# Attention and low-rank mixer: the halves of an odd pair's product with values put closer together, both transposes of a couple asked for at once

## Chip, cores, metric

The kernel runs on one core of a Trainium2 chip. The metric is device time in microseconds (us), lower is better. All runs were of a granted TensorE clock (the share of full speed that the chip allowed) of 0.996 to 1.000 as the mean of a run.

## The reference, cut to what matters

```python
q_n = q / (norm(q) + 1e-06); k_n = k / (norm(k) + 1e-06)      # 8 batches, 12 heads, 448 rows, 64 wide
attn = softmax(q_n @ k_n.T / tau)
x = (attn @ v).transpose(0, 2, 1, 3).reshape(8, 448, 768)
u = x + (x.transpose(0, 2, 1) @ U @ V).transpose(0, 2, 1)       # rank 32
out = u + maximum(u @ w_ch1, 0) @ w_ch2                         # 768 -> 3072 -> 768
```

## The kernel before

TensorE works on pairs of heads, six to a batch: pair n is pair p = n mod 6 of batch b. From n = 14 on, two pairs (an even one and the odd one after it) make a couple. Between the steps of attention, the kernel puts pieces of the mixer of the batch before ("channel pieces", six matmuls each, taken from the list `fill`), so that TensorE never runs dry. `V(n, half)` is a half of the product with values and its division (the result is X), `A2` the product U^T X for a couple, `X2` the request for X's transpose, `T` the request for a transposed q and k, `S3` the last chunk of the scores.

```python
def spread(n, order, nf, first=0):
    weights = [w if fn is not False else 0 for w, fn in order]
    given = acc = 0
    for i, ((_, fn), w) in enumerate(zip(order, weights)):
        if fn:
            fn()
        for g in after.pop((n, i + first), []):
            g()
        acc += w
        want = nf * acc // sum(weights)          # whole pieces
        f(min(want - given, len(fill)))
        given = want
# ... (even pair of a couple)
order = [
    (3, lambda: (step_S3(*pairs[n]), Sc(n, 0, 1))),
    (2, lambda: V(n - 1, 0)),
    (3, lambda: (V(n - 1, 1), X2(n - 1))),
    (4, lambda: (A2(n - 2), Sc(n, 2), Sc(n + 1, 0), open_V(*pairs[n]))),
    (2, lambda: V(n, 0)),
    (3, lambda: (V(n, 1), X2(n))),
]
spread(n, order, int(round((len(fill) - KEEP) / (1 + (-p) % NP))))
# ... (where the norms of a later couple are made: reduce of q, reduce of k, root; then invert)
at = [(m - 3, 0), (m - 3, 0), (m - 3, 5)] + [(m - 2, i) for i in (0, 1, 2)]
when = (m - 2, 3)
# ... (accumulator banks of the channel pieces: two, in turn; U^T X takes the other one)
def own_bank():
    other = 1 - m_state["at"]
    if not m_state["open"]:
        m_state["at"] = other
    return bank_m(other)
# ...
def step_A2(b, p, apart):
    ap = own_bank()[:, 0:128] if apart else av_of[(b, p + 1, 1)][:, 384:512]
    # ... eight matmuls of U_sb and X, then
    nc.scalar.copy(out=A_of[(b, p)], in_=ap)
```

## Time and profile before

| | before |
|---|---|
| time, median of 4 runs | 579.82 us (579.45 to 580.06) |
| span of the profiled run | 578.5 us |
| TensorE busy | 567.5 us, 98% |
| VectorE, ScalarE busy | 212.9 us, 262.6 us |

The prediction below shows the lines that matter. In the wait lines, the columns are the engine and line that waited, what it waited for, then the sum, the number and the longest of such waits.

### The profile page before, as it was taken

To read this page: it belongs to the slowest core of one execution; us is meant where nothing else is said; L and a number is where in the kernel's file an instruction comes from. 1 tells how busy PE (TensorE), PEld (TensorE's weight loads), DVE (VectorE), ACT (ScalarE), POOL (GpSimd) and SP (SyncE) were. 2 spreads that over 40 slices of the span, in tenths; PEclk is the share of its full clock that TensorE was granted. 3 is DMA by queue.
4 is the path that set the end of the run, shared out by engine and by line. 5 is a ranking of instruction groups with operands and counts; after the bars stand their busy time and mean duration, and the time that the engine had idled before them with its cause. 6 is when DMAs were issued, how large, how long until landed. Compare 5 with 4: busy or idle time off the path is not lost.

```text
span 578.5 us, 12651 instructions
## 1 busy us (share of the span) xinstructions
PE 567.5 (98%) x5302; PEld 330.3 (57%) x5302; DVE 212.9 (37%) x460; ACT 262.6 (45%) x449; POOL 214.0 (37%) x202
## 2 busy tenths in 40 slices
PE   6999999999999999999999999999999999999997
PEld 6665566555655556555556555655565555655565
DVE  7874551433343324524234233333243331320011
ACT  5877544465333662445424555336433365214300
POOL 8756574724416236416145064244161420000000
PEclk9999999999999999999999999999999999999999
DMA  6899999686367565574465673674545612222022
GB/s 163 191 245 240 233 209 205 174 170 153 95 139 146 108 141 124 127 160 110 92 151 135 130 151 99 139 167 98 116 112 126 139 38 50 57 54 51 7 49 56
DMA packets 139882, 74.53 MB, mean 129 GB/s; under 512 B 86688, under 2 KB 139696, under 8 KB 139824
## 3 DMA queue, kind: packets, MB, share of 16 engines
q1 hardware_dynamic: 129568, 63.20, 48.9%
q0 software_dynamic: 9632, 10.01, 10.2%
q8 instruction: 41, 0.67, 0.5%
q10 hardware_dynamic: 624, 0.51, 0.3%
q14 instruction: 17, 0.14, 0.1%
HBM read 52.19 MB, written 11.01 MB: 109 GB/s over the span
## 4 chain that ended last, share of the span: by engine, by line
PE 83%; DMA 8%; DVE 3%; SPq 2%; POOL 1%; ACT 1%; issue 1%; POOLq 0%; DVEq 0%
PE mp L598 34%; PE mp L570 33%; PE sc L331 5%; DMA w_sb<-in_moe_w_ch_dram 5%; DMA kst<-in_k_dram 2%; PE av L419 2%; PE up L419 1%; PE av L393 1%; PE up L393 1%; PE av L343 1%; POOL sq L243 1%; SPq L315 1%; PE mp L508 1%; ACT E L356 1%; DVE ss L248 1%
## 5 line engine op out<-in xcount | busy, mean ns | idle before, releaser
L598 PE MATMUL mp<-w_sb,relu 128*128 128x384 bf16 (+2 forms) x1368 | 235.3, 323 | 0.3 <-DMA w_sb<-in_moe_w_ch_dram 0.3
L598 PEld LDWEIGHTS <-relu 128*128 128x128 bf16 x1368 | 126.1, 98 | 84.1 <-issue 9.6
L570 PEld LDWEIGHTS <-w_sb 128*128 128x128 bf16 x1128 | 105.8, 98 | 99.3 <-issue 7.2
L356 ACT ACTIVATE E<-sc 128x896 bf16<-128x896 f32 x144 | 125.1, 922 | 53.4 <-PE sc L331 52.4
L575 ACT ACTIVATE relu<-mp 128x448 bf16<-128x448 f32 x163 | 88.7, 544 | 122.1 <-PE mp L570 122.1
L268 POOL TENSOR_TENSOR qk<-kst,inv 128x512 bf16<-128x512 f32 x43 | 46.0, 1069 | 236.7 <-DVE inv L262 215.2
L570 PE MATMUL mp<-uO,w_sb 128*128 128x448 bf16 x576 | 113.6, 353 | 0.0
L570 PE MATMUL mp<-uE,w_sb 128*128 128x448 bf16 x552 | 111.9, 353 | 0.2 <-DMA w_sb<-in_moe_w_ch_dram 0.2
L617 DVE TENSOR_TENSOR o_sb<-mp,ut 128x384 f32<-128x384 f32 (+2 forms) x51 | 28.0, 550 | 140.1 <-PE mp L598 140.1
L248 DVE TENSOR_REDUCE ss<-sq 128x16 f32<-128x1024 f32 (+1 forms) x50 | 57.7, 1165 | 1.6 <-POOL sq L243 0.8
L577 DVE TENSOR_SCALAR relu<-mp 128x448 bf16<-128x448 f32 x25 | 15.6, 625 | 99.5 <-PE mp L570 99.0
L268 POOL TENSOR_TENSOR qk<-qst,inv 128x512 bf16<-128x512 f32 x44 | 47.4, 1079 | 1.7 <-PE up L480 1.7
L331 PE MATMUL sc<-qkT 64*64 64x448 bf16 x576 | 42.8, 360 | 0.6 <-ACT E L356 0.3
L243 POOL TENSOR_TENSOR sq<-kst 128x1024 f32<-128x1024 f32 (+1 forms) x23 | 42.7, 1857 | 1.6 <-DMA kst<-in_k_dram 1.4
L243 POOL TENSOR_TENSOR sq<-qst 128x1024 f32<-128x1024 f32 x21 | 39.8, 1893 | 7.3 <-DMA qst<-in_q_dram 6.3
L276 POOL CAST v<-vst 128x1024 bf16<-128x1024 f32 (+1 forms) x25 | 25.2, 1010 | 11.8 <-DMA vst<-in_v_dram 10.4
L419 PEld LDWEIGHTS <-E 128*128 128x128 bf16 x744 | 29.1, 97 | 0.0
L353 ACT ACTIVATE E<-av 128x448 bf16<-128x448 f32 x17 | 9.2, 541 | 42.4 <-PE up L343 21.8
L331 PEld LDWEIGHTS <-qkT 64*64 64x64 bf16 x576 | 12.8, 105 | 14.2 <-issue 8.6
L393 PEld LDWEIGHTS <-E 128*128 128x128 bf16 x408 | 17.3, 97 | 5.0
L419 PE MATMUL av<-v,E 128*128 128x65 bf16 x420 | 18.9, 193 | 0.0
L412 PEld LDWEIGHTS <-E 128*128 128x128 bf16 x124 | 11.4, 98 | 9.0 <-issue 0.8
(109 smaller groups left out, 364.9 us busy)
## 6 DMA issues: line engine op xcount, KB each, us to landing
out_dram<-o_sb SPq DMA_DIRECT2D x108, 96.0 KB, 2.2
w_sb<-in_moe_w_ch_dram POOLq DMA_DIRECT2D x8, 1152.0 KB, 18.4
qst<-in_q_dram SPq DMA_DIRECT2D x23, 256.0 KB, 3.9
vst<-in_v_dram SPq DMA_DIRECT2D x46, 128.0 KB, 2.8
kst<-in_k_dram SPq DMA_DIRECT2D x44, 128.0 KB, 2.9
qst<-in_q_dram SPq DMA_DIRECT2D x23, 192.0 KB, 4.0
vst<-in_v_dram SPq DMA_DIRECT2D x46, 96.0 KB, 2.7
kst<-in_k_dram SPq DMA_DIRECT2D x44, 96.0 KB, 2.8
```

The lines of the kernel that those rows point to most:

```text
L243: nc.gpsimd.tensor_mul(sq[:, 0:self.nh * 4, :], self.flat(t), self.flat(t))
L248: nc.vector.reduce_sum(self.ss[:, j, 0:self.nh * 4], self.sq[j][:, 0:self.nh * 4, :], axis=AX.X)
L268: eng.tensor_mul(qks[self.gi % 2][:, j, i, :, :, :], t[:, 2 * j:2 * j + 2, :, :].rearrange("p h c d -> p c h d"), iv.unsqueeze(3).to_broad ...
L276: nc.gpsimd.tensor_copy(out=self.flat(v65[self.s])[:, :, 0:D], in_=self.flat(vst[self.s]))
L331: nc.tensor.matmul(out=sc[o:o + 64, h, 0:S], lhsT=t[r, 1, c * 128 + o:c * 128 + o + 64], rhs=t[r, 0, 0:S], start=True, stop=True)
L356: nc.scalar.activation(out=e[:, 2 * c:2 * c + 2, 0:S], in_=sc[:, :, 0:S], func=AF.Exp)
L393: nc.tensor.matmul(out=av[:, ic, :], lhsT=e[:, 2 * c + h, ic * 128:(ic + 1) * 128], rhs=vv[:, 2 * j + h, c, :], start=False, stop=(ic == 3 ...
L419: nc.tensor.matmul(out=av[:, i, h, :], lhsT=e[:, 2 * c + h, ic * 128:(ic + 1) * 128], rhs=vv[:, 2 * j + h, c, :], start=False, stop=(i == ...
L570: nc.tensor.matmul(out=mp, lhsT=w1_sb[:, cc, f * 128:(f + 1) * 128], rhs=u[:, cc, 0:S], start=(cc == 0), stop=(cc == CC - 1))
L575: nc.scalar.activation(out=relu[:, f, o:o + S], in_=mp, func=AF.Relu)
L598: nc.tensor.matmul(out=mp, lhsT=relu[:, f, r0:r0 + 128], rhs=w2_sb[:, f, half * HC + c0:half * HC + c1], start=(f == 0), stop=(b > 0 and f ...
L617: nc.vector.tensor_add(o.rearrange("p (k d) -> p k d", d=128), mp.rearrange("p (k d) -> p k d", d=128), ut_of[(b, half)][:, c0 // 128:c1 / ...
```

## The change

The intent: a half of the odd pair's product with values should come sooner, so that its division on VectorE is done when U^T X needs X, with two channel pieces between them instead of one; and both transposes of a couple should be asked for together.

```diff
@@ requests for transposes
-            put(m - 1, -1 if first else 0, lambda m=m: T(m + 1))
+            put(m - 1, -1, lambda m=m: T(m + 1))
@@ order of an even pair
-                (2, lambda: V(n - 1, 0)),
-                (3, lambda: (V(n - 1, 1), X2(n - 1))),
+                (1, lambda: V(n - 1, 0)),
+                (4, lambda: (V(n - 1, 1), X2(n - 1))),
```

## The prediction

> **What bounds the kernel now.** I began with the page's busy table and its slices. They say that TensorE is never idle for long, at full granted clock, in all forty slices.
>
> ```profile
> PE 567.5 (98%) x5302; PEld 330.3 (57%) x5302; DVE 212.9 (37%) x460; ACT 262.6 (45%) x449; POOL 214.0 (37%) x202
> ...
> PEclk9999999999999999999999999999999999999999
> ```
>
> No other engine is above 45%, so only what stands in TensorE's own stream, or what its stream waits for, can move the end. Next I read the waits of TensorE. In the part that the change touches (from about 190 us on) there are only two kinds: two stalls of U^T X (L508) for X, and one of the scores for a transposed qkT.
>
> ```profile
> PE up L343 <- DMA qkT<-qk: 0.4, 1, 0.4
> PE mp L508 <- DVE X L431: 0.4, 2, 0.2
> ```
>
> These waits look like the aim of the change. Third, I opened the timeline around one of the two X stalls (columns: start, duration, engine, line, what, and in brackets the idle time before).
>
> ```profile
> 235.12 1.14 PE L598 MATMUL mp<-w_sb,relu 128*128 128x384 bf16 x6
> 235.88 1.21 DVE L248 TENSOR_REDUCE ss<-sq 128x16 f32<-128x1024 f32 x1
> 237.01 0.55 DVE L617 TENSOR_TENSOR o_sb<-mp,ut 128x384 f32<-128x384 f32 x1
> 237.47 0.17 DVE L430 RECIPROCAL rd<-up 128x4 f32<-128x4 f32 x1
> 237.66 0.29 PE L508 MATMUL mp<-X,U_sb 128*32 128x128 bf16 x6
> 237.68 0.42 DVE L431 TENSOR_TENSOR X<-up,rd 128x256 bf16<-128x256 f32 x1
> 238.16 0.23 PE L508 MATMUL mp<-X,U_sb 128*32 128x128 bf16 x2 [0.20 <-DVE X L431]
> 238.32 0.57 PE L331 MATMUL sc<-qkT 64*64 64x448 bf16 x8
> ```
>
> The last two of eight matmuls wait for the second half of X, which ends at 237.68 + 0.42 = 238.10; it was late because VectorE ran a reduce and the output addition (L617) first. From the first L508 to the scores it took 238.32 - 237.66 = 0.66 us. Where nothing waits (at 218.73) the same stretch takes 218.96 - 218.73 = 0.23. So one stall costs 0.43 us, not the 0.20 in the brackets, and the two together 0.86.
>
> **What the Trainium skill says.** "Perfetto Trace Analysis", Tensor Engine Instruction, says the recorded end of a matmul is a model, not a measurement; so I measure by starts alone. The trace agrees: six channel matmuls of 384 columns are recorded as 1.14 us, but start to start (235.12 to the next product's 236.10) they take 0.98. "PSUM — Partial Sum Buffer", Engine vs sequencer instructions, says that ScalarE's and VectorE's queues are strict FIFO and that matmuls start in program order. This trace agrees where L617 stands ahead of the division above. The same page, PSUM bank collisions raise a hardware error, advises guarding PSUM by bank: a product can't open a bank until the engine that empties it is done. That is the rule on which my prediction turns.
>
> **The change part by part.** I compared the two built programs, engine by engine, with their semaphores and wait values.
>
> *The transposes.* Asking for T(m+1) one place earlier gives no different program: with this line alone changed, every engine's instructions, semaphores and wait values are the same as before, because nothing else for the DMA queue stands between the two places. So it is worth 0, and the 0.4 us wait on qkT stays.
>
> *The halves.* The weights 2,3 become 1,4, but steps are whole numbers. With 9 steps to a pair (in even batches) the rounding gives the same order. With 7 steps (the mixer of the even batch before has 24 + 24 steps to spread over six pairs) it gives 0,2 channel pieces behind the halves in place of 1,1. The order of TensorE differs in eight places only, each moving one piece of six matmuls from between the halves to behind them. Call them by the pair p: p=2 in batches 3, 5, 7 (about 194, 330 and 466 us), p=4 in the same (216, 351, 488), p=0 in batches 4 and 6 (235, 370). No matmul is added or taken away, and the first quarter of the trace shows halves back to back without loss: their first matmuls at 22.70 and 23.20 are 0.50 apart, the same 0.50 that a half takes with a piece behind it (215.69 to 216.19). So without waits U^T X would start at the same time as before. What is left is what it waits for.
>
> It starts after two pieces, in the accumulator bank of the first of the two, so that piece must be emptied from the bank. Before, that first piece lay one half earlier. Now its emptying stands later in the queue of VectorE or ScalarE.
>
> (a) p=0, two places. VectorE now divides before L617. The division starts after the reduce, at 237.01, and its multiply 0.21 later at 237.22 (237.68 - 237.47); L617 follows 0.34 after that (238.02, the next instruction, less 237.68), at 237.56, and takes 0.56, to 238.12. The X stall is gone: X is whole by 237.64. But in the changed program the first L508 waits for L617. Instruction end to matmul start was 238.16 - 238.10 = 0.06, so it starts at 238.18, and the scores 0.23 later at 238.41, against 238.32 before. Loss 0.09; the other place (373.30) works out to 0.10. The wait for X has been swapped for one on the output addition; net **+0.2 us** for two, where 0.86 was to be saved.
>
> (b) p=2, three places. Here the pieces are of the first product and ScalarE empties the first with relu (L575). Before:
>
> ```profile
> 196.19 0.54 ACT L575 ACTIVATE relu<-mp 128x448 bf16<-128x448 f32 x1 [0.53 <-PE mp L570]
> ...
> 196.90 0.32 ACT L253 ACTIVATE ss<-ss,tiny 128x32 f32<-128x32 f32 x1 [0.16 <-DVE ss L248]
> ...
> 197.25 0.23 ACT L254 ACTIVATE ss<-ss 128x32 f32<-128x32 f32 x1
> ...
> 197.72 0.30 PE L508 MATMUL mp<-X,U_sb 128*32 128x128 bf16 x8
> ```
>
> In the changed program this relu stands behind L253 and L254, the square root of the norms, which waits for a VectorE reduce that does not move (ends 196.86). The piece itself would be done near 196.66, but relu has to stand in line: ScalarE's next instruction starts about 0.11 before the recorded end of the last (18.37 + 0.92 against 19.18), so relu runs from 197.37 to 197.91, and L508 starts 0.05 to 0.06 later at 197.96 instead of 197.72: loss 0.24. The places at 333.35 and 469.50 have the same distances. Three of them, **+0.7 us**.
>
> (c) p=4, three places. The pieces are quarters of one accumulation (L598) with nothing to empty between them; the reduce still holds the division, X still ends at 218.73 and the last two L508 still find it. **0**.
>
> All of it lies in TensorE's stream, which is full to the end, so it adds straight to the time: 0.2 + 0.7 = 0.9 us. 579.99 + 0.9 = **580.9 us**, 0.16% slower.
>
> **The rivals.** *The intended gain.* The two stalls for X go and nothing replaces them: 580.0 - 0.9 = 579.1. For it: the stalls are real, and VectorE does divide sooner. Against it: the wait values of the changed program put L617 before L508 and the root before relu. *Nothing at all*, 580.0: the eight shifts are absorbed. For it: each is a quarter of a microsecond and a run's spread was 0.6; against it: the only slack in the stream after these places is the one 0.4 us wait on qkT at 439. If a delayed TensorE gives that transfer time, up to 0.4 comes back, 580.5; but the transfer's queue follows TensorE's own output, so I expect both to shift together. *A cascade.* A_sb, the exponentials and the next half's inputs on ScalarE come 0.25 late, and the next products wait again, doubling (b): 581.7. Against it: these exponentials wait for the scores, which are late by the same amount, so distances are kept.
>
> **Range and chances.** The sizes are from one trace with an error of perhaps 0.1 us a place; a different chip or run moved the before kernel by 0.6. Low end just under half of the intended gain, high end the cascade: 579.5 to 581.7. A change of 2% would be 11.6 us, more than all of TensorE's idle time (578.5 - 567.5 = 11.0), so faster by 2% has practically no chance, and nothing adds so much either: 0.01, 0.98, 0.01.
>
> **What would show it.** Right: the wait of L508 for X is gone, with two of about 0.4 us for L617's o_sb and three of about 0.2 for relu L575 in its place; the wait of L343 for qkT still there; L508 to scores 0.23 in all eight places. Wrong, if no wait of L508 is listed and the span is shorter by most of 0.9; or if the p=4 places change; or if waits appear later, at L331, L393 or L419, which would be the cascade.

## The result

The changed kernel took 581.77 us, median of 4 runs (581.02 to 582.80), against 579.82 of before: 1.95 us more. The ratio was 1.0035, 95% interval 1.0015 to 1.0055. (A ratio is the mean time of one kernel's fast runs over that of the other's of the same rounds, so it is not quite the ratio of the medians.) The time is within 2% as forecast, but 581.77 lies above the range of 579.5 to 581.7, and the loss is about twice the 0.9 us predicted.

The busy time of TensorE did not move. First the page of the changed kernel, then TensorE's waits in it:

```profile
PE 567.5 (98%) x5302; PEld 330.7 (57%) x5302; DVE 213.0 (37%) x460; ACT 262.7 (45%) x449; POOL 214.1 (37%) x202
```

```profile
PE mp L570 <- DMA w_sb<-in_moe_w_ch_dram: 1.1, 1, 1.1
PE mp L598 <- DMA w_sb<-in_moe_w_ch_dram: 0.9, 1, 0.9
PE mp L508 <- DVE o_sb L617: 0.8, 2, 0.4
...
PE mp L508 <- ACT relu L575: 0.5, 3, 0.2
...
PE up L343 <- DMA qkT<-qk: 0.3, 1, 0.3
```

The third and fourth lines are the predicted ones: the two waits for X have gone, two for the output addition and three for relu have come. The first two were not in the prediction. In the kernel before the same two waits are short:

```profile
PE mp L598 <- DMA w_sb<-in_moe_w_ch_dram: 0.3, 1, 0.3
...
PE mp L570 <- DMA w_sb<-in_moe_w_ch_dram: 0.2, 1, 0.2
```

They fall at 55 and 80 us, far ahead of the first changed instruction at about 194 us, in a stretch whose program is the same in both kernels.

The timeline of the changed kernel at a p=2 place (start, duration, engine, line, what, idle before it). Both halves now precede two pieces in a row:

```profile
196.93 2.43 PE L570 MATMUL mp<-uE,w_sb 128*128 128x448 bf16 x12
...
198.47 0.32 ACT L253 ACTIVATE ss<-ss,tiny 128x32 f32<-128x32 f32 x1 [1.24 <-DVE ss L248]
...
198.83 0.23 ACT L254 ACTIVATE ss<-ss 128x32 f32<-128x32 f32 x1
...
198.96 0.98 ACT L575 ACTIVATE relu<-mp 128x448 bf16<-128x448 f32 x2
...
199.54 0.29 PE L508 MATMUL mp<-X,U_sb 128*32 128x128 bf16 x8 [0.18 <-ACT relu L575]
```

ScalarE stands idle for 1.24 us ahead of the root L253, which waits for a reduce. Relu comes only after both parts of the root, and U^T X waits for it, though the first piece was ready before the root: in root_between below, relu starts 1.33 us after its piece (197.99 less 196.66), which would be 198.26 here, an estimate. And at a p=0 place:

```profile
237.50 2.11 PE L598 MATMUL mp<-w_sb,relu 128*128 128x384 bf16 x12
...
237.76 1.21 DVE L248 TENSOR_REDUCE ss<-sq 128x16 f32<-128x1024 f32 x1
...
238.89 0.17 DVE L430 RECIPROCAL rd<-up 128x4 f32<-128x4 f32 x1
...
239.09 0.42 DVE L431 TENSOR_TENSOR X<-up,rd 128x256 bf16<-128x256 f32 x1
...
239.44 0.55 DVE L617 TENSOR_TENSOR o_sb<-mp,ut 128x384 f32<-128x384 f32 x1
...
240.04 0.29 PE L508 MATMUL mp<-X,U_sb 128*32 128x128 bf16 x8 [0.42 <-DVE o_sb L617]
```

X is whole at 239.51, half a microsecond ahead, but the bank that U^T X writes is only emptied at 239.99.

### A ledger of each profile

To see where a profile's time lies, I cut it into three. The **start** is where the first U^T X begins; up to there (and on to 190 us) the tested kernels run the same program except where an experiment says otherwise. The **qkT stalls** are the extra time near 303 and 438 us: from the first matmul of S3 to the next channel piece takes 0.69 us where no transfer is late, and what is over is the stall. The **rest** is the span less both.

| profile | span | start | qkT stalls | rest |
|---|---|---|---|---|
| before | 578.5 | 104.00 | 0.30 + 0.81 | 473.39 |
| changed | 581.0 | 105.53 | 0.47 + 0.64 | 474.36 |
| transposes_only (same program as before) | 578.8 | 104.30 | 0.61 + 0.58 | 473.31 |
| halves_only (same program as changed) | 578.9 | 104.40 | 0 + 0.29 | 474.21 |
| after_again (the changed kernel) | 580.4 | 105.20 | 0.38 + 0.43 | 474.39 |
| root_between | 579.5 | 105.30 | 0.36 + 0.31 | 473.53 |
| p0_only | 578.3 | 104.02 | 0.44 + 0.41 | 473.43 |
| after_reduce | 576.8 | 103.69 | 0.47 + 0.22 | 472.42 |
| before_reduce | 576.9 | 103.83 | 0 + 0.59 | 472.48 |
| w2_late | 578.1 | 103.49 | 0.53 + 0.72 | 473.36 |
| early_T | 579.2 | 105.83 | 0 + 0 | 473.37 |
| together | 576.3 | 103.90 | 0 + 0 | 472.40 |

The rest repeats within 0.2 us for kernels that should be alike. Of the 2.5 us between the first two profiles, 1.53 lie in the start, 0 in the qkT stalls and 0.97 in the part that was changed.

### The profile page after: what moved, and what is told of

Read it like the earlier page. It is cut to its first block, busy times and chain, and to the rows that moved or that the text cites. A ratio compares the mean times of both kernels' runs of the same rounds, so it can differ in the third digit from the quotient of the medians.

```text
span 581.0 us, 12651 instructions
## 1 busy us (share of the span) xinstructions
PE 567.5 (98%) x5302; PEld 330.7 (57%) x5302; DVE 213.0 (37%) x460; ACT 262.7 (45%) x449; POOL 214.1 (37%) x202
## 4 chain that ended last, share of the span: by engine, by line
PE 81%; DMA 9%; DVE 4%; SPq 3%; ACT 2%; issue 1%; POOL 1%; DVEq 0%; POOLq 0%; ACTq 0%
PE mp L598 34%; PE mp L570 32%; DMA w_sb<-in_moe_w_ch_dram 5%; PE sc L331 5%; DMA qst<-in_q_dram 2%; PE av L419 2%; DMA kst<-in_k_dram 1%; DVE ss L248 1%; DMA qkT<-qk 1%; PE av L393 1%; PE up L419 1%; PE up L393 1%; PE av L343 1%; PE mp L508 1%; DVE X L431 1%
## 5 line engine op out<-in xcount | busy, mean ns | idle before, releaser
L598 PE MATMUL mp<-w_sb,relu 128*128 128x384 bf16 (+2 forms) x1368 | 234.4, 323 | 0.9 <-DMA w_sb<-in_moe_w_ch_dram 0.9
L598 PEld LDWEIGHTS <-relu 128*128 128x128 bf16 x1368 | 126.4, 98 | 85.3 <-issue 10.2
L570 PEld LDWEIGHTS <-w_sb 128*128 128x128 bf16 x1128 | 106.0, 98 | 100.7 <-issue 7.2
L570 PE MATMUL mp<-uO,w_sb 128*128 128x448 bf16 x576 | 113.6, 353 | 0.0
L570 PE MATMUL mp<-uE,w_sb 128*128 128x448 bf16 x552 | 111.4, 353 | 1.1 <-DMA w_sb<-in_moe_w_ch_dram 1.1
L243 POOL TENSOR_TENSOR sq<-kst 128x1024 f32<-128x1024 f32 (+1 forms) x23 | 42.6, 1856 | 0.5 <-DMA kst<-in_k_dram 0.3
L419 PEld LDWEIGHTS <-E 128*128 128x128 bf16 x744 | 29.1, 97 | 0.0
L393 PEld LDWEIGHTS <-E 128*128 128x128 bf16 x408 | 17.3, 97 | 5.0
L430 DVE RECIPROCAL rd<-av 128x4 f32<-128x4 f32 x35 | 6.2, 177 | 28.5 <-PE av L419 28.5
```

Of the source, the lines that this page charges most:

```text
L243: nc.gpsimd.tensor_mul(sq[:, 0:self.nh * 4, :], self.flat(t), self.flat(t))
L393: nc.tensor.matmul(out=av[:, ic, :], lhsT=e[:, 2 * c + h, ic * 128:(ic + 1) * 128], rhs=vv[:, 2 * j + h, c, :], start=False, stop=(ic == 3 ...
L419: nc.tensor.matmul(out=av[:, i, h, :], lhsT=e[:, 2 * c + h, ic * 128:(ic + 1) * 128], rhs=vv[:, 2 * j + h, c, :], start=False, stop=(i == ...
L570: nc.tensor.matmul(out=mp, lhsT=w1_sb[:, cc, f * 128:(f + 1) * 128], rhs=u[:, cc, 0:S], start=(cc == 0), stop=(cc == CC - 1))
L598: nc.tensor.matmul(out=mp, lhsT=relu[:, f, r0:r0 + 128], rhs=w2_sb[:, f, half * HC + c0:half * HC + c1], start=(f == 0), stop=(b > 0 and f ...
```

## The experiments

All were correct and timed in five rounds. transposes_only, halves_only, root_between and after_reduce ran together on one chip; after_again, p0_only, before_reduce and w2_late on another; early_T and together on that other one again. Each ratio is to the kernel before on the same chip. "Changed" is the kernel with the diff above.

### transposes_only: the second part of the change alone

```diff
 kernel before
-            put(m - 1, -1 if first else 0, lambda m=m: T(m + 1))
+            put(m - 1, -1, lambda m=m: T(m + 1))
```

> The kernel before with only the transposes asked for together. Its built program is the same as that of before, waits included, so this is a test of before against itself. My theory: ratio to before 1.000, waits of U^T X for X (0.4 us, two) as before, the wait of the scores for qkT still there. Rival (the transposes matter): the qkT wait goes and the time falls by 0.4 us or more. For the start: the stretch up to the first U^T X (at 104.00 in the trace of before, 105.53 in that of the changed kernel), whose program is the same in both, should move by up to 1.5 us from run to run if it is chance; if the shift belongs to the program, this run shows 104.0.

Measured: 579.90 us (579.56 to 580.62, 6 runs), ratio 0.9993 (0.9980 to 1.0007). Both X stalls and the qkT stalls are there, the start lies at 104.30. The built program is that of before, so this part of the change is worth nothing, and what moved between these two profiles (0.3 in the start, 0.08 in the qkT stalls) moved by chance.

### halves_only and after_again: the changed program measured again

```diff
 halves_only: changed kernel (after_again is the changed kernel itself)
-            put(m - 1, -1, lambda m=m: T(m + 1))
+            put(m - 1, -1 if first else 0, lambda m=m: T(m + 1))
```

> The changed kernel without the transposes; its built program is the same as that of the changed kernel, so it is a second, independent measurement of it. My theory: waits of U^T X for o_sb (0.8 us, two) and relu (0.5 us, three); from the first U^T X to the end 0.9 us longer than before; over many rounds 0.9 us slower in all (ratio 1.0016), because the further 1.5 us of the first changed profile stood ahead of the first changed instruction and should come and go. Rival (the early shift belongs to the changed program): the first U^T X again at 105.5 and the ratio again 1.0035.

> The changed kernel once more, with many rounds. My theory: the waits for o_sb and relu as in its first profile; the time from the first U^T X (near 104) to the end is the same within the stalls on qkT, and where the first U^T X lies between 103.7 and 105.5 follows the longest landing of a w2 load (33.0 us where it was 103.7, 35.0 where 105.5). Ratio to before 1.001 to 1.002. Rival (the changed program is really 2 us slower): ratio 1.0035 again.

Measured: halves_only 580.72 us (580.47 to 581.76, 6 runs), ratio 1.0010 (0.9997 to 1.0023); after_again 580.90 us (579.97 to 582.21, 6 runs), ratio 1.0010 (0.9998 to 1.0023). Both show the two waits for o_sb and the three for relu. The start came at 104.40 in the one and 105.20 in the other. So the ratio of 1.0035 did not repeat, though its interval and the later ones overlap. Over all its runs the changed program has a mean of 581.17 us (16 runs) against 580.16 of before (27 runs): 1.0 us. The first four runs, with a mean of 581.84, were high ones; the twelve later have 580.94. The kernel before has such runs as well: it goes up to 581.71. Its own first four, with a mean of 579.79, were low ones; the 23 later have 580.22.

### root_between: relu ahead of the root again

```diff
 changed kernel; order[2] is the second half with its weight of 4
-            spread(n, order, int(round((len(fill) - KEEP) / (1 + (-p) % NP))))
+            nf = int(round((len(fill) - KEEP) / (1 + (-p) % NP)))
+            if nf == 7:
+                order[2:3] = [(2, order[2][1]), (2, None)]
+                for i in (5, 4, 3, 2):
+                    if (n, i) in after:
+                        after[(n, i + 1)] = after.pop((n, i))
+            spread(n, order, nf)
```

> The changed kernel with the root of the norms put between the two channel pieces at the three p=2 places, so that the relu of the first piece stands ahead of it on ScalarE, as before; nothing else in the program differs. My theory: the three waits for relu (0.5 us listed, 0.25 each in the alignment) are gone, the two for o_sb (0.8) stay; from the first U^T X to the end 0.7 us shorter than the changed kernel. Rival (the order of TensorE itself costs time): no change against the changed kernel.

The edit makes the root come after the first of the two pieces. It acts wherever a pair has 7 pieces, at p=0 and p=4 too; there the first piece has no relu, and in the trace the root stays where it was on ScalarE.

ScalarE and TensorE in its timeline at the first p=2 place:

```profile
197.99 0.54 ACT L575 ACTIVATE relu<-mp 128x448 bf16<-128x448 f32 x1 [1.02 <-PE mp L570]
...
198.43 0.31 ACT L253 ACTIVATE ss<-ss,tiny 128x32 f32<-128x32 f32 x1
...
199.02 0.30 PE L508 MATMUL mp<-X,U_sb 128*32 128x128 bf16 x8
```

No wait for relu is left, and from the last half's final group of matmuls to the scores it takes 2.96 us where the changed kernel takes 3.21: 0.25 at each of the three places. The rest is 473.53, against 474.32 as the mean of the three profiles of the changed program: 0.79 less, as expected. TensorE's order is that of the changed kernel, so the order itself doesn't cost this. The measured time (580.66 us, ratio to before 1.0005, interval 0.9990 to 1.0019) is too coarse to show it.

### p0_only: the change at two places alone

```diff
 kernel before
-                (2, lambda: V(n - 1, 0)),
-                (3, lambda: (V(n - 1, 1), X2(n - 1))),
+                (1 if p == 0 else 2, lambda: V(n - 1, 0)),
+                (4 if p == 0 else 3, lambda: (V(n - 1, 1), X2(n - 1))),
```

> The kernel before with the change at the two p=0 places alone. My theory: the two waits of U^T X for X (0.4 us listed) become two for o_sb (0.8 us listed), no wait for relu; each of the two places 0.1 us longer than in before, 0.2 in all, too little for the clock. Rival (the change does help where X was late): the two places become shorter by 0.4 each.

Measured: 580.07 us, ratio 1.0001 (0.9989 to 1.0013). The two waits for X became two for o_sb, and each of the two places takes 0.06 us longer than in before (3.14 less 0.98 for the piece that now comes after the half, against 2.10). Smaller than the 0.1 that was expected, but the sign holds: one stall has replaced another.

### after_reduce and before_reduce: the reduce out of the way

```diff
 changed kernel (after_reduce), kernel before (before_reduce)
-            at = [(m - 3, 0), (m - 3, 0), (m - 3, 5)] + [(m - 2, i) for i in (0, 1, 2)]
+            at = [(m - 3, 0), (m - 3, 0), (m - 3, 5)] + [(m - 2, i) for i in (0, 0, 2)]
```

> The changed kernel with the second reduce of a couple's norms one place earlier, into idle time of VectorE ahead of the first half; TensorE's order is exactly that of the changed kernel. My theory: division, output addition and root all come early enough; no wait of U^T X is left at the eight places, neither for X nor for o_sb nor for relu; from the first U^T X to the end 0.9 us shorter than before and 1.8 us shorter than the changed kernel; total about 0.998 of before. Rival (the reduce then holds a relu or a division elsewhere): new waits of L570 or L598 of the same size.

> The kernel before, halves not moved, with the second reduce of the norms one place earlier. My theory: the order of the halves is worth nothing by itself once the reduce is out of the way, so this gives the same as the changed kernel with the early reduce: no wait of U^T X at the eight places, first U^T X to the end 0.9 us shorter than before less what the stalls on qkT give, ratio about 0.998. Rival (two pieces of distance are needed as well): some waits of U^T X for X stay and the time is nearer to before.

The timeline of after_reduce at the first p=0 place:

```profile
231.19 2.33 DVE L248 TENSOR_REDUCE ss<-sq 128x16 f32<-128x1024 f32 x2
...
235.70 0.42 DVE L431 TENSOR_TENSOR X<-up,rd 128x256 bf16<-128x256 f32 x1
...
236.41 0.56 DVE L617 TENSOR_TENSOR o_sb<-mp,ut 128x384 f32<-128x384 f32 x1 [0.28 <-PE mp L598]
...
237.27 0.30 PE L508 MATMUL mp<-X,U_sb 128*32 128x128 bf16 x8
```

Both reduces now run in time that VectorE had idle. X is done at 236.12 and the output addition at 236.97, and nothing waits. Neither kernel has a wait of U^T X for X, o_sb or relu at any of the eight places. after_reduce: 578.74 us (578.36 to 580.04), ratio 0.9979 (0.9964 to 0.9993). before_reduce: 579.15 us (578.40 to 581.22), ratio 0.9986 (0.9971 to 1.0000). The rests are 472.42 and 472.48, 0.9 under before and 1.9 under the changed program. With the reduce gone from the queue, the order of the halves is worth nothing that one profile of each can show: 0.06 us between the two.

### w2_late: the start

The start is later where TensorE waits for weights, and there are two such waits. The first, of L570 near 55 us, is for a load of the first layer's weights (w1); it rose from 0.2 to 1.1 us. GpSimd issued that load 2.5 us later, behind a cast of v that waited for v to land; TensorE went on 11.2 us after the issue (55.97 less 44.73), which is the least time to landing among the four w1 loads of that profile. Before, then changed:

```profile
41.27 1.04 POOL L276 CAST v<-vst 128x1024 bf16<-128x1024 f32 x1 [2.35 <-DMA vst<-in_v_dram]
42.26 0.87 POOL L168 DMA_DIRECT2D w_sb<-in_moe_w_ch_dram  x1
```

```profile
43.49 1.29 POOL L276 CAST v<-vst 128x1024 bf16<-128x1024 f32 x1 [4.01 <-DMA vst<-in_v_dram]
44.73 0.87 POOL L168 DMA_DIRECT2D w_sb<-in_moe_w_ch_dram  x1
```

This divides the twelve profiles. In changed, after_again, root_between and early_T the w1 load was issued at 44.4 to 45.0 and the start came at 105.2 to 105.8; in the other eight at 42.0 to 42.6, with the start at 103.5 to 104.4. Each of these four profiled runs is the slowest of its kernel's timed runs; of the other eight only transposes_only's is. This is read from the traces; no experiment moved the load.

The second wait, of L598 near 80 us, is for the second layer's weights (w2); it rose from 0.3 to 0.9. The last line of the view of that load's source line (least, median and most time from issue to landing, over four loads), before and changed:

```profile
DMA to landing us min/median/max: 22.6/27.3/33.4
```

```profile
DMA to landing us min/median/max: 23.6/28.7/35.0
```

The same loads, the first issued at 50.1 and 50.2 us, took up to 1.6 us longer to land. The experiment tests this second wait alone.

```diff
 kernel before
-    put(NP + 1, 2, lambda: (load_w2(1, 0, 12), load_w2(1, 12, 24)))
+    put(NP + 2, 2, lambda: (load_w2(1, 0, 12), load_w2(1, 12, 24)))
```

> The kernel before with the second half of w2 asked for one pair later, so that the first half has the transfers to itself for longer. For the start only: if the landing of w2's first half sets where the first U^T X lies, its longest landing falls under 33 us, the waits of L598 for w_sb go, the first U^T X comes at 103.7 or earlier and the runs scatter less (within 0.6 us in place of 2.3). Rival (the scatter comes from the first 20 us, or from the total of bytes): the scatter stays, or L598 waits for the second half later on.

```profile
DMA to landing us min/median/max: 20.5/25.1/28.3
```

Half met. The longest landing fell to 28.3 us, no wait for w_sb is left, and the start came at 103.49, the earliest of all. But the w1 load was an early one here (42.0); after_reduce has no wait for w_sb either with the w2 loads in their old place (start 103.69), and together, which has this diff, still waits 0.4 us for them. So it is not shown that the edit moved the start. The runs scatter about as before, 579.29 to 581.09, and the time did not fall measurably (580.06 us, ratio 0.9998, interval 0.9986 to 1.0010).

### early_T and together: the qkT stalls, and a faster kernel

```diff
 kernel before (early_T); together has also the diffs of before_reduce and w2_late
-            put(*((m - 2, 6) if first else (m - 1, -1)), lambda m=m: T(m))
-            put(m - 1, -1 if first else 0, lambda m=m: T(m + 1))
+            at = (m - 2, 5) if m > 2 * NP + 2 else (m - 1, -1)
+            put(*((m - 2, 6) if first else at), lambda m=m: T(m))
+            put(*((m - 1, -1) if first else at), lambda m=m: T(m + 1))
```

> The kernel before with both transposes of a couple asked for really earlier: right behind the request for XT at the end of the pair before, ahead of the output stores that stood in the DMA queue before them. My theory: the stalls of the scores on qkT near 303 and 438 us (0.7 to 1.3 us together in the profiles so far, different in each run) are gone and stay gone; about 0.9 us shorter than before (ratio 0.9985), the two X stalls of U^T X stay. Rival (the transfer itself sets when qkT is there, not its place in the queue): the stalls stay.

> The kernel before, halves not moved, with the early reduce, the early transposes and the second half of w2 asked for later. My theory: the savings add: 0.9 (no stall of U^T X) and 0.9 (none on qkT) and some 0.3 at the start: about 578.0, ratio 0.9965; no wait of L508 or L343 listed. Rival (the waits hide one another): not below the kernel with the early reduce alone, 0.998 to 0.9986.

The DMA queue in before, then in early_T, ahead of the stall at 438:

```profile
431.26 2.00 SPq L500 DMA_TRANSPOSE XT<-X  x1
433.30 0.59 SPq L623 DMA_DIRECT2D out_dram<-o_sb  x1
433.93 0.59 SPq L627 DMA_DIRECT2D out_dram<-o_sb  x1
434.64 2.65 SPq L315 DMA_TRANSPOSE qkT<-qk  x2
```

```profile
432.74 1.66 SPq L500 DMA_TRANSPOSE XT<-X  x1
434.51 2.62 SPq L315 DMA_TRANSPOSE qkT<-qk  x2
```

The two output stores no longer stand between XT and the transposes. S3 came at 438.41 in before and at 439.89 in early_T, whose whole run was later from the start, so relative to TensorE the request came 1.6 us sooner. No qkT stall is left in either kernel. (Near 303 that also happened by itself, in halves_only and before_reduce, so the two stalls together range lower, from 0.29, than the 0.7 of the expectation; near 438 no other profile is under 0.22.) early_T: 579.32 us, ratio 0.9987 (0.9974 to 1.0001), so the time alone doesn't show the gain. together: 578.67 us (578.11 to 578.98, 4 runs), ratio 0.9975 (0.9961 to 0.9990), with a rest of 472.40; it is the fastest of all medians, though not apart from after_reduce by more than their scatter. In the ledger the savings add as expected (against before 0.99 in the rest and 1.11 in the qkT stalls; at the start 0.1 where 0.3 was hoped for). By the time it is open: the ratio is weaker than the expected 0.9965, which lies inside its interval, and the rival, not below the kernel with the early reduce alone, is not excluded.

early_T's profile shows a second source of a late start. Eight matmuls of the scores in before and in early_T:

```profile
10.29 0.57 PE L331 MATMUL sc<-qkT 64*64 64x448 bf16 x8 [0.17 <-DVE qkT L305]
```

```profile
10.97 0.96 PE L331 MATMUL sc<-qkT 64*64 64x448 bf16 x8
```

The same work is recorded at 0.96 us instead of 0.57, and by 15.5 us this run was 0.76 us late. The trace shows the granted clock lower there: 0.50 from 10.0 to 13.4 us, where the other eleven profiles have 1.00 all the way from 8 to 16 us (`prof early_T --windows`). What lowered it, no run here settles. The mean of this run was 0.997; so was that of the slowest run of before (581.71), which was not profiled.

## Why the prediction was right or wrong

**The transposes are worth 0.** Right, by the identical built program and by transposes_only.

**p=2: ScalarE's root ahead of relu, 0.7 us.** Right: 0.25 at each of three places (0.24 predicted), 0.79 in the ledger by root_between.

**p=0: the wait for X is swapped for one on the output addition, +0.2.** Right in kind, a little large: 0.06 at each place where 0.09 and 0.10 were predicted.

**p=4: 0.** Right: 2.65 us from the half to the scores at all three, of which 0.98 is the moved piece, against 1.67 or 1.68 before.

**Sum.** The rest rose from 473.36 (mean of the four profiles that keep before's waits: before, transposes_only, w2_late, early_T) to 474.32 (mean of three): 0.96 where 0.9 was predicted. No rival took place: no gain, no absorption and no cascade.

**The step that failed is the one from the trace to the measured time**: "a different chip or run moved the before kernel by 0.6". The mechanism and the sizes of the change came out; the allowance around them was too small. That 0.6 was the spread of three runs, and 27 runs of the same kernel spread over 2.3 us (579.43 to 581.71). In the profiles the start moves (103.5 to 105.8), and so do the stalls on qkT (0.29 to 1.25 in all where they were not taken away). The first changed profile had a late start: 1.53 us, more than the change itself cost, lay ahead of the first changed instruction, with a w1 load issued 2.5 us later and w2 loads that landed up to 1.6 us later.

The four runs that gave 581.77 were about 0.9 us higher on average than the twelve later runs of the same program (581.84 against 580.94). Close to half of the first loss, then, belonged to no instruction of the change, and a range around a known 0.9 us had to hold this scatter too. That the same late start lies behind the other high runs fits, but only one run of each kernel has a profile, so it isn't shown. The four were also unusually high: of the 495 ways to take four of the twelve later runs, nine have a median of 581.77 or more.

**A smaller slip:** the prediction counted one stall on qkT of 0.4 us from the list of TensorE's waits. There were two, and they cost 1.11 us in that profile; the one near 303 is listed under the weight loads alone.

**What stays open:** why v and the weights land late in some runs, why the granted clock fell in early_T, and whether the changed program starts late more often (105.53, 104.40 and 105.20 in its three profiles; of the five profiles with the halves moved at all eight places three start late, of the seven others one). Against it: the program of that stretch is the same, early_T starts at 105.83 with the halves not moved, and after_reduce, with TensorE's order of the changed kernel, shows 103.69. Twelve profiles can't settle it.

## What to carry to other kernels

When work is moved to give a value more time, list everything that the consumer waits for, its output bank included, and follow the queue of the engine that frees that bank: here X came half a microsecond early and the bank came late. Look for what blocks the queue (a reduce that could run in idle time) before reordering the saturated engine; that gained 0.9 us in the ledger with either order. And where effects are below 1 us, repeat the unchanged kernel often enough to know its scatter, and compare profiles from a mark after the start.

## What the Trainium skill lacked or had wrong

- "Perfetto Trace Analysis", Tensor Engine Instruction, says that a matmul's end is modelled; it doesn't say what follows for waits. An idle time listed at 0.20 us cost 0.43 us from start to start, and the qkT stall at 438 was listed at 0.4 and cost 0.81.
- "TensorE: Matmul & The Clock Gate", Back-to-back issue gap, gives a measured sustained spacing of about 131 ns for 512 columns, and N/2.4 + 2.5 ns for a matmul by itself. Here a stream of weight loads and matmuls of 448 columns took 1.13 us for six (194.86 to 195.99 in the kernel before), 188 ns each. This agrees with the second formula (189 ns, an estimate from it) and not with the first figure, which is smaller although it is for more columns.
- No page that I drew on says how much the landing of one and the same load varies from run to run: 33.0 to 35.0 us for the slowest w2 load over the profiles with the loads in their old place.
